# Spreading z over the partitions: one float32 product, or two float32r products of its halves

## Chip, core and metric

The kernel runs on one core of one Trainium2 chip. The metric is the device time of one execution in microseconds (us). Before the change three runs gave 1108.91, 1110.42 and 1110.47 us; the median is 1110.42 us.

## The reference

Random-feature attention over 8 batches, 8 heads, 576 tokens of 64 dimensions with 128 features, then a gated product with two weight matrices and an output matrix:

```python
    q_p, k_p = (phi(q_s), phi(k_s))          # exp(proj - sq - max) / sqrt(m), float32
    kv = np.einsum('bhsm,bhsd->bhmd', k_p, v)
    z = np.sum(k_p, axis=2)
    num = np.einsum('bhsm,bhmd->bhsd', q_p, kv)
    den = np.einsum('bhsm,bhm->bhs', q_p, z)[..., None] + 1e-06
    ...
    return (a * b @ w_out).astype(np.float32)   # a = x @ w_a, b = x @ w_b, x = num / den
```

`z` is the sum of the key features over the tokens of one head: 128 numbers per head. The denominator of every query token is its dot product with `z`.

## The kernel before

**Two kinds of work.** Attention is done by pairs of heads: `pair(u)`, u from 0 to 31, four pairs to a batch. The matrix products after it are done by blocks: `moe_block` for batches 0 and 1, and `moe_block7` (seven products of sub-blocks in place of eight) for batches 2 to 7 and for a last block 8, which holds the 64 left-over tokens of every batch. While block b runs, the pairs of batch b+1 are computed beside it. Blocks 2 to 6 each carry four pairs of the next batch, blocks 7 and 8 carry none.

**Number formats.** The block products split each operand into a rounded float32r part and the float32r rest and make three products (`hi*hi`, `hi*lo`, `lo*hi`). `copier` (L268 on ScalarE, L270 on VectorE) makes the rounded part, `subber` (L276, VectorE) the rest. Attention products are plain float32; the compiler turns each into two TensorE instructions.

**One pair from u = 4 on.** The features of keys (`hk`) and queries (`hq`) come from TensorE (L479), a maximum on VectorE (L502) and an exponential on ScalarE (L515). Then `zadd` (L531) sums the key features over the token chunks with six additions on GpSimd; the result `zs` holds, for each partition, its partial sum of the two heads (128 partitions x 256 numbers). At L540 one float32 product with `ones` (128 x 128, all 1.0) adds the 128 partial sums and puts the total on every partition: `pz`, in PSUM. ScalarE copies it to `zb` (L268). VectorE then makes the denominators `dn` from `hq` and `zb` (L579 to L585), ScalarE scales `hq` (L590), VectorE turns 32x32 blocks (L600), four DMAs write it to `qdr` and one reads it back (L610), and `pm` (L621) is the numerator product, already divided. `split` makes the float32r parts of x from `pm`, and `sums` (L409) the sub-block sums S for `moe_block7`. The pairs 0 to 3 (`u < NFAST`) take another way, `tok_tail`, that has no `zs` and no `pz`. The features lie in a ring of three buffers (`H=3`): a pair needs two, so pair u starts when pair u-2 has read its `hq` in `pm` and pair u-1 its `hk` in `pkv` (L554).

**What sets the order.** Nothing is ordered by hand. `Graph.op` notes each operation with its engine, its cost in ns, its inputs, its buffers and a priority; `Graph.schedule` simulates the five engines and always places the operation that can start first, the lower priority number on a tie. Attention of pair u has priorities near 1000 u, block products start at one million, so attention goes first when both are ready. The order found is then issued; at run time each engine works through its own list in that order. Costs that matter here: `mm4(1, 256)` = 434 ns for the float32 product, `mm(2, 256)` = 240 ns for two float32r products, `act(256)` = 385 ns, `dve(256)` = 416 ns, 738 and 458 ns for the additions on GpSimd, and 70 ns (`LAT`) for each hand-over from one engine to another. `margin` holds an operation back after its inputs are ready: 2200 ns for `pz` (`MARGIN` 1200 + `SUMS` 1000). `GATES` ties the start of the pairs of a batch to units -1, 1, 3 and 5 of the twelve units of a block.

**Output products.** The products `o` (L739) need only the hidden values of a finished unit, so a few of them are always left over and are placed wherever TensorE would wait (`flush`). Twelve groups of three are left over at the end of a block.

Of the kernel before, what the change touches and what calls it, by code (L numbers as in the profile page):

```python
# [7 lines left out]
F32 = mybir.dt.float32  # L8
F32R = mybir.dt.float32r
# [5 lines left out]
X = mybir.AxisListType.X  # L15
PSUM = bass.MemoryType.PSUM

P = 128
B, H, S, D, M = 8, 8, 576, 64, 128
NHP = H // 2  # L20
NU = B * NHP
E, FF = H * D, 1536
NF = FF // P
# [7 lines left out]
VW = D + 2  # L31
# [2 lines left out]
SQ = (0.5 / float(D) ** 0.5) ** 0.5  # L34
EPS = 1e-6 * M

CFG = dict(NFAST=4, H=3, TURN=(7,), BACK=300, AT=2, GATES=(-1, 1, 3, 5), SQPE=4, MARGIN=1200, LOAD=2500, SUMS=1000, JOIN=(0, 1, 2), CONV=(28000, 2600))

# [169 lines left out]
def mm4(n, cols):  # L210
    return n * 2 * max(112, 3 + 0.835 * cols)


def dve(n):
    return 150 + 1.04 * n


def act(n):
    return 165 + 0.86 * n
# [10 lines left out]
@with_exitstack  # L230
def tile_attention_moe(ctx: ExitStack, tc: tile.TileContext, kqt, kqn, vx, omst, idn, wab, wout, out):
    nc = tc.nc
    NFAST, SQPE = CFG["NFAST"], CFG["SQPE"]
    const = ctx.enter_context(tc.tile_pool(name="const", bufs=1))
    sp = ctx.enter_context(tc.tile_pool(name="sp", bufs=1))
    ps = ctx.enter_context(tc.tile_pool(name="ps", bufs=1, space=PSUM))
# [4 lines left out]
        return ap.bitcast(F32)  # L241

    g = Graph()
    for name, n in dict(X=2, Xw=0, nat=2, x2=0, v=2, h=CFG["H"], qd=1, kvz=0, sm=2, sq=2, rd=2, x=4, xa=2, xf=2, S=2, st=0,
                        w=NF, u=NF, t=0, tst=0, wo=3, raw=2, a=2, c=0, bq=0, ghl=2, osb=0, zs=1, z2=1, zb=1, k2=1, kl=2, dn=1, tails=0,
                        at=CFG["AT"], ab=2, o=4).items():
        g.ring(name, n)

    IN_U = dict(st=["u0", "u1"], t=[f"u{k}" for k in range(2, 7)], c=["u7", "u8", "u9"], xa=["u10", "u11"],
                tst=["S0", *(f"u{k}" for k in range(NF))], bq=["a0", "a1"], osb=["raw0", "raw1"])  # L250
# [6 lines left out]
    def fixed(shape, dtype, name):  # L257
        b = g.buf(None, shape, dtype, name)
        b.ap = const.tile(shape, dtype, name=name)
        return b  # L260
# [3 lines left out]
    def copier(o, i, scale=None):  # L264

        def go(e):
            if e == "ACT":
                nc.scalar.copy(o(), i())  # L268
            elif e == "DVE":
                nc.vector.tensor_copy(o(), i())  # L270
            else:
                nc.gpsimd.tensor_scalar(o(), i(), 1.0, 0.0, op0=ALU.mult, op1=ALU.add)
        return go

    def subber(o, i, hi):
        return lambda e: ENG[e].tensor_tensor(o(), i(), f(hi()), op=ALU.subtract)  # L276
# [4 lines left out]

    ident = fixed([P, P], F32, "ident")
    om = fixed([P, M], F32, "om")
    ones = fixed([P, P], F32, "ones")
    junk = fixed([P, M], mybir.dt.bfloat16, "junk")
    ind = fixed([P, 2], F32, "ind")
    for k in range(4):
        g.op({"POOL": 110}, lambda e, k=k: nc.gpsimd.memset(ind.ap[D * (k // 2):D * (k // 2) + D, k % 2:k % 2 + 1], float(k in (0, 3))),
             w=[(ind, k)], prio=-5000)
# [39 lines left out]
    for n, (kind, i, w) in enumerate(units):  # L329
        pr = 4000 + n * 4000 / len(units)  # L330
        more = late[:10] if n < 18 else []
        raw = g.buf("raw", [P, NW], I64 if wide else F32, f"raw{n}", more)
# [3 lines left out]
        if kind == "ab":  # L336
            hb = wab_b[i, w] = g.buf("wu"[i % 2], [P, 2, NC4, P], F32R, f"w{'ab'[w]}{i}")
            v = lambda hb, k: hb.ap[:, k].rearrange("p c f -> p (c f)")
        else:
            hb = wo_b[i] = g.buf("wo", [P, 2, E], F32R, f"wo{i}")  # L340
            v = lambda hb, k: hb.ap[:, k]
# [78 lines left out]

    def pair(u, gate):
        b, hp = divmod(u, NHP)
        nm, pr, fast = f"_{b}_{hp}", 1000 * u, u < NFAST
        more = ["ab0", "ab1", "o0", "o1", "o2", "o3"] if u < NHP else []
        mg = 0 if u < NHP else CFG["MARGIN"]

# [16 lines left out]
        for xb, (c0, c1) in zip(xbs, pieces):  # L443
            g.op({"SP": 330}, dma(lambda xb=xb: xb.ap[:], lambda c0=c0, c1=c1: kqt[b, hp][:, c0 * P:c1 * P]), w=[(xb, None)], alloc=[xb],
                 prio=early, nbytes=P * (c1 - c0) * P * 4)
        h = {}
        if u >= SQPE:
            nat = [g.buf("nat", [P, NCH, D], F32, f"nat{'kq'[w]}{nm}", room) for w in range(2)]
# [6 lines left out]
        if u >= SQPE:  # L455
            sq = g.buf("sq", [P, 2, NCH], F32, f"sq{nm}")
            for w in range(2):
                g.op({"ACT": act(NCH * D)}, lambda e, w=w: nc.scalar.activation(nat[w].ap[:], nat[w].ap[:], AF.Square, scale=SQ),
                     r=[(nat[w], None)], w=[(nat[w], None)], prio=pr, margin=0 if u < 2 * NHP else CFG["LOAD"])
                g.op({"DVE": dve(NCH * D)}, lambda e, w=w: nc.vector.tensor_reduce(sq.ap[:, w], nat[w].ap[:], axis=X, op=ALU.add),  # L460
                     r=[(nat[w], None)], w=[(sq, w)], alloc=[sq] if w == 0 else [], prio=pr)
# [63 lines left out]
        zs = g.buf("zs", [P, 2, M], F32, f"zs{nm}")  # L525
        zb = g.buf("zb", [P, 2, M], F32, f"zb{nm}")
        z2 = g.buf("z2", [P, 2, M], F32, f"z2{nm}")
        pri = pr + 40
# [3 lines left out]
        for j in range(2):  # L532
            c0, tr = 5 * j, slice(TL * j, TL * j + TL)
            zadd("POOL", 2 * M, lambda: z2.ap[:], lambda c0=c0: hk.ap[:, c0:c0 + 2], lambda c0=c0: hk.ap[:, c0 + 2:c0 + 4],
                 [(hk, c0 + i) for i in range(4)], [(z2, None)], [z2, zs] if j == 0 else [])
            zadd("POOL", M, lambda j=j: zs.ap[:, j], lambda: z2.ap[:, 0], lambda: z2.ap[:, 1], [(z2, None)], [(zs, j)])
            zadd("POOL", M, lambda j=j, tr=tr: zs.ap[tr, j], lambda j=j, tr=tr: zs.ap[tr, j], lambda tr=tr: hk.ap[tr, 4],
                 [(zs, j), (hk, 4)], [(zs, j)])
        pz = g.buf("at", [P, 2 * M], F32, f"pz{nm}", more)
        g.op({"PE": mm4(1, 2 * M)}, lambda e: nc.tensor.matmul(pz.ap[:], ones.ap[:], zs.ap.rearrange("p j m -> p (j m)"), start=True, stop=True),  # L540
             r=[(zs, None), (ones, None)], w=[(pz, None)], alloc=[pz, zb], prio=pri + 10, margin=mg and mg + CFG["SUMS"])
        g.op({"ACT": act(2 * M)}, copier(lambda: zb.ap.rearrange("p j m -> p (j m)"), lambda: pz.ap[:]), r=[(pz, None)], w=[(zb, None)], prio=pri + 10)

        k2 = g.buf("k2", [P, M], F32, f"k2{nm}")
# [18 lines left out]
        kl = g.buf("kl", [P, 2, D], F32, f"kl{nm}")  # L563
# [3 lines left out]
        hq = h[1]  # L567

        dn = g.buf("dn", [P, NCH], F32, f"dn{nm}")
        pri = pr + 100  # L570
# [16 lines left out]
        for c in range(NCH):  # L587
# [3 lines left out]
                else:  # L591
                    nc.gpsimd.tensor_scalar(hq.ap[:, c], hq.ap[:, c], dn.ap[:, c:c + 1], None, op0=ALU.mult)
            g.op({"ACT": 392}, scale, r=[(hq, c), (dn, None)], w=[(hq, c)], prio=pri)
        if u in CFG["TURN"]:
            t = pe_transposes(nm, pr, mg, more, hq)
            qT = t, lambda j: t.ap[:, 5 * j:5 * j + 4], lambda j: t.ap[:, 4, TL * j:TL * j + TL]
        else:

            qd = g.buf("qd", [P, 4, NCH, 32], F32, f"qd{nm}")
            g.op({"DVE": dve(NCH * M)}, lambda e: nc.vector.transpose(qd.ap[:], hq.ap.rearrange("p c (j r) -> p j c r", r=32)),  # L600
                 r=[(hq, c) for c in range(NCH)], w=[(qd, None)], alloc=[qd], prio=pr + 110)
            view = lambda: hq.ap.rearrange("p c m -> p (c m)").rearrange("p (i c r) -> p i c r", c=NCH, r=32)


            qdr = qdram[u % 3]
            back = qdram_b[u % 3]

            def spread(e):
                for i in range(4):
                    nc.sync.dma_start(qdr[:, :, i].rearrange("j r n -> r j n"), qd.ap[32 * i:32 * i + 32].rearrange("p j c r -> p j (c r)"))  # L610
            g.op({"SP": 2000}, spread, r=[(qd, None)], w=[(back, None)], prio=-30, nbytes=P * NCH * M * 4)
            g.op({"SP": 400}, dma(lambda: hq.ap.rearrange("p c m -> p (c m)"), lambda: qdr.rearrange("j r i n -> (j r) (i n)")), r=[(back, None)],
                 w=[(hq, None)], prio=-30, nbytes=P * NCH * M * 4, margin=CFG["BACK"])
            qT = hq, lambda j: view()[:, :, 5 * j:5 * j + 4].rearrange("p i c r -> p c i r"), lambda j: view()[:, 2 * j:2 * j + 2, 4]
# [10 lines left out]
        def rest(pt):  # L625
# [2 lines left out]
            g.op({"ACT": act(TL)}, copier(lambda: xT.ap[:, hp, tl], lambda: pt.ap[:, M:M + TL]), r=[(pt, None)], w=[(xT, (hp, b))], prio=pri)  # L628
        me = dict(mm=num, rest=rest, cost=mm4(1, SM) + mm4(1, TL), r=[(kl, None), (qT[0], None)],
                  w=[(pm, None)], alloc=[pm, *xt.new])  # L630
        if hp in CFG["JOIN"]:
            pending.append(me)
        else:
            pt = g.buf("at", [P, M + TL], F32, f"pt{nm}", more)
            g.op({"PE": me["cost"] + 290}, lambda e: num(pt), r=me["r"], w=[*me["w"], (pt, None)], alloc=[pt, *me["alloc"]], prio=pri, margin=mg)
            rest(pt)

    def pe_transposes(nm, pr, mg, more, hq, room=()):

        qb = g.buf("qd", [P, NCH, P], F32, f"qT{nm}", room)  # L640
        for i in range(3):
            pq = g.buf("at", [P, 3 * P], F32, f"pq{nm}{i}", more)

            def go(e, i=i, pq=pq):
                for c in range(3):
                    nc.tensor.transpose(pq.ap[:, c * P:(c + 1) * P], hq.ap[:, 3 * i + c], ident.ap[:])
            g.op({"PE": 3 * 108}, go, r=[(ident, None), *((hq, 3 * i + c) for c in range(3))], w=[(pq, None)], alloc=[pq, qb] if i == 0 else [pq],
                 prio=pr + 110 + 10 * i, margin=mg)
            g.op({"ACT": act(3 * P), "DVE": dve(3 * P) + 100}, copier(lambda i=i: qb.ap[:, 3 * i:3 * i + 3].rearrange("p c t -> p (c t)"), lambda pq=pq: pq.ap[:]),
                 r=[(pq, None)], w=[(qb, i)], prio=pr + 110 + 10 * i)  # L650
        return qb

    def tok_tail(b, hp, nm, pr, mg, more, vb, h, xt):

        hk = h[0]
        kvz = g.buf("kvz", [P, 2, VW], F32, f"kvz{nm}", ["zs0"])
        x32t = g.buf("xf", [P, 4, 2, D], F32, f"x32t{nm}")
        pkv = g.buf("at", [P, 2, 2 * VW + 2], F32, f"pkv{nm}", more)
        heads = [[(0, 0), (1, 1), (2, 2), (3, 3), (4, 4)], [(4, 5), (5, 6), (6, 7), (7, 8), (8, 9)]]
# [9 lines left out]
        g.op({"PE": mm4(10, VW)}, kvmm, r=[(vb, None), (hk, None)], w=[(pkv, None)], alloc=[pkv, kvz], prio=pr + 100, margin=mg)  # L669
        g.op({"ACT": act(2 * VW)}, copier(lambda: kvz.ap[:], lambda: pkv.ap[:, :, 0:VW]), r=[(pkv, None)], w=[(kvz, None)], prio=pr + 100)  # L670
        qT = pe_transposes(nm, pr, mg, more, h[1], ["S1"])
        tails = g.buf("tails", [P, 2, D], F32, f"tails{nm}", ["z20"])
        for j in range(2):
            pn = g.buf("at", [P, 5, WN], F32, f"pn{nm}{j}", more)
            rd = g.buf("rd", [P, 5], F32, f"rd{nm}{j}")
# [338 lines left out]
```

## Time and profile before

| | |
|---|---|
| median of three runs | 1110.42 us |
| profiled execution: time | 1111.44 us |
| profiled execution: span from first to last instruction | 1109.6 us |
| time around the span | 1.84 us |
| TensorE busy | 1088.2 us, 98% |
| VectorE busy | 815.4 us, 73% |
| ScalarE busy | 562.1 us, 51% |
| GpSimd busy | 105.2 us, 9% |
| granted TensorE clock | 0.994 of full |

PE is TensorE's matmul, PEld its weight load, DVE VectorE, ACT ScalarE, POOL GpSimd. Every duration below comes from this one profiled execution. The time around the span does not depend on the kernel's inner order, so a change of the span is carried over to the median as it is. The stages by time: 0 to 97.5 us holds the pairs of batch 0, the start of block 0 and the conversion of the weights; 97.5 to about 201 us the rest of block 0 with the pairs 4 to 7; then block 1 with pairs 8 to 11 to 321.5 us; blocks 2 to 6 of 118.6 to 119.0 us each; blocks 7 and 8 from 915.5 us to the end.

### The profile page before, as it was taken

The page shows a single profiled execution, that of the slowest core. Times are in us where ns is not written, and L with a number is a line of the kernel's source. Part 1 is how long each engine was busy: PE and PEld are TensorE (multiplying, and loading weights), DVE is VectorE, ACT ScalarE, POOL GpSimd, SP SyncE. Part 2 cuts the span into 40 slices and gives each one's busy share as a digit, 9 for nine tenths or more (in the row PEclk, how much of TensorE's full clock was granted, in tenths as well). Part 3 has the DMA queues.
Part 4 walks back from the last instruction along what each step waited for, and adds up shares of the span by engine and source line. Part 5 has one row for each costly group of instructions (what it writes and reads, how often), then busy time and mean ns, then how long its engine had stood idle before and what let it go on. Part 6 is the DMA issues. An engine that isn't in the chain of part 4 may idle for free.

```text
span 1109.6 us, 21421 instructions
## 1 busy us (share of the span) xinstructions
PE 1088.2 (98%) x7717; PEld 938.5 (85%) x7717; DVE 815.4 (73%) x2052; ACT 562.1 (51%) x1544; POOL 105.2 (9%) x176
## 2 busy tenths in 40 slices
PE   8989999999999999999999999999999999999997
PEld 7877777777779888888888898888889889999996
DVE  4799786888978677877697778778877676556544
ACT  5787575766556555554465546564655521002001
POOL 0002010111011111111011111111111100000000
PEclk9899999999999999999999999999999999999999
DMA  9555775697989887888888888888887678777763
GB/s 343 170 196 178 243 226 193 219 341 273 307 284 310 303 285 266 297 287 297 270 268 302 288 284 286 308 294 271 277 298 239 226 260 268 237 245 253 262 226 84
DMA packets 106826, 290.36 MB, mean 262 GB/s; under 512 B 11744, under 2 KB 29664, under 8 KB 106720
## 3 DMA queue, kind: packets, MB, share of 16 engines
q1 hardware_dynamic: 106432, 288.86, 77.2%
q8 instruction: 61, 1.00, 0.3%
q14 instruction: 45, 0.37, 0.1%
q10 hardware_dynamic: 288, 0.13, 0.0%
HBM read 241.57 MB, written 47.38 MB: 260 GB/s over the span
## 4 chain that ended last, share of the span: by engine, by line
PE 86%; DVE 7%; DMA 4%; issue 2%; ACT 1%; SPq 0%; DVEq 0%; ACTq 0%
PE p L875 37%; PE o L739 25%; PE ppk L479 6%; PE pb L785 4%; PE pa L785 4%; PE pkv L554 3%; PE pm L621 2%; DVE raw L315 1%; PE pz L540 1%; DMA raw<-in_wab_dram 1%; DVE sm L502 1%; PE pkv L668 1%; PE ps L492 1%; DMA hq<-qdr 1%; DMA td<-ts 1%
## 5 line engine op out<-in xcount | busy, mean ns | idle before, releaser
L739 PE MATMUL o<-wo,ghl 128*128 128x512 f32 x1296 | 350.7, 399 | 0.0
L885 DVE TENSOR_TENSOR c<-p,c 128x512 f32<-128x512 f32 (+1 forms) x336 | 208.3, 620 | 152.0 <-PE p L875 146.8
L739 PEld LDWEIGHTS o<-wo,ghl 128*128 128x128 f32 x1296 | 226.2, 188 | 38.8
L875 PE MATMUL p<-S,t 128*128 128x256 f32 x1512 | 209.8, 283 | 0.0
L875 PEld LDWEIGHTS p<-S,t 128*128 128x128 f32 x1512 | 194.4, 189 | 9.2
L531 POOL TENSOR_TENSOR z<-hk 128x256 f32<-128x256 f32 x56 | 46.1, 823 | 765.8 <-ACT hk L515 653.5
L479 PE MATMUL ppk<-om,X 64*128 64x128 f32 x576 | 92.0, 295 | 4.3 <-DMA om<-in_omst_dram 3.9
L479 PEld LDWEIGHTS ppk<-om,X 64*128 64x128 f32 x576 | 73.4, 192 | 26.0 <-issue 6.9
L268 ACT COPY c<-p 128x256 f32<-128x256 f32 x84 | 30.9, 368 | 126.2 <-PE p L875 126.2
L590 ACT ACTIVATE hq<-hq,dn 128x128 f32<-128x128 f32 x252 | 78.3, 393 | 32.6 <-DVE dn L585 29.0
L515 ACT ACTIVATE hk<-hk,sm 128x128 f32<-128x128 f32 x216 | 71.6, 393 | 43.6 <-DVE sm L510 42.9
L479 PE MATMUL ppq<-om,X 64*128 64x128 f32 x576 | 91.8, 295 | 0.0
L579 DVE CUSTOM_DVE_ANT_0 junk<-hq,zb 128x128 bf16<-128x128 f32 (+1 forms) x280 | 80.6, 288 | 10.4 <-ACT zb L268 5.9
L785 PE MATMUL pa<-x,wa 128*128 128x512 f32 x288 | 76.3, 405 | 3.1 <-DVE x L276 2.6
L785 PE MATMUL pb<-x,wb 128*128 128x512 f32 x288 | 76.4, 404 | 0.0
L268 ACT CAST ghl<-c 128x512 fp32r<-128x512 f32 x52 | 32.1, 619 | 87.4 <-DVE c L920 86.7
L875 PEld LDWEIGHTS p<-x,t 128*128 128x128 f32 x504 | 69.5, 188 | 6.2
L875 PE MATMUL p<-x,t 128*128 128x256 f32 x504 | 73.9, 282 | 0.0
L875 PE MATMUL p<-S,bq 128*128 128x256 f32 x504 | 73.8, 282 | 0.0
L479 PEld LDWEIGHTS ppq<-om,X 64*128 64x128 f32 x576 | 73.3, 192 | 0.2 <-DVE x L276 0.2
L875 PEld LDWEIGHTS p<-x,wa 128*128 128x128 f32 x504 | 66.4, 188 | 7.8 <-DVE c L885 3.1
L515 ACT ACTIVATE hq<-hq,sm 128x128 f32<-128x128 f32 x216 | 72.5, 390 | 0.0
(120 smaller groups left out, 1644.0 us busy)
## 6 DMA issues: line engine op xcount, KB each, us to landing
t<-td SPq DMA_DIRECT2D x168, 512.0 KB, 4.8
wo<-wod SPq DMA_DIRECT2D x96, 512.0 KB, 5.1
bq<-bd SPq DMA_DIRECT2D x84, 256.0 KB, 5.2
X<-in_kqt_dram SPq DMA_DIRECT2D x28, 576.0 KB, 5.2
qdr<-qd SPq DMA_DIRECT2D x108, 144.0 KB, 3.6
hq<-qdr SPq DMA_DIRECT2D x27, 576.0 KB, 6.2
raw<-in_wab_dram SPq DMA_DIRECT2D x24, 512.0 KB, 4.6
td<-ts SPq DMA_DIRECT2D x24, 512.0 KB, 6.3
```

Source lines behind the costliest of these rows:

```text
L268: nc.scalar.copy(o(), i())
L479: nc.tensor.matmul(pps[w].ap[:, c * M:c * M + M], xcol(3 * i + c)[rows], om.ap[rows], start=True, stop=True)
L515: g.op({"ACT": 392}, lambda e, c=c, w=w, src=src[w]: nc.scalar.activation(h[w].ap[:, c], src(c), AF.Exp, scale=SC, bias=sm.ap[:, 2, w, c:c ...
L531: g.op({"POOL": pool2(n)}, lambda e: ENG[e].tensor_tensor(o(), a(), c(), op=ALU.add), r=r, w=w, alloc=list(al), prio=pri)
L554: nc.tensor.matmul(pkv.ap[D * j:D * j + D, 0:M], vb.ap[:, vc, 0:D], hk.ap[:, c], start=(n == 0), stop=(n == 4))
L579: g.op({"DVE": 413}, lambda e, c=c, j=j, rr=rr: nc.vector.tensor_tensor_reduce(out=junk.ap[rr], in0=hq.ap[rr, c], in1=zb.ap[rr, j], scale= ...
L590: nc.scalar.activation(hq.ap[:, c], hq.ap[:, c], AF.Copy, scale=dn.ap[:, c:c + 1])
L621: nc.tensor.matmul(pm.ap[D * j:D * j + D], kl.ap[:, j], qT[1](j), start=True, stop=True)
L739: nc.tensor.matmul(po.ap[:], ghl.ap[:, gi, t * P:(t + 1) * P], wo.ap[:, wi], start=(n == 0 and i == 0), stop=(n == NF - 1 and i == 2))
L785: nc.tensor.matmul(pb.ap[:], wt.ap[:, wi, c], xs[c].at(xi), start=(c == 0 and i == 0), stop=(c == NC4 - 1 and i == 2))
L875: nc.tensor.matmul(pb.ap[:, half], wcol(wi, c), xc(xi, c), start=n == 0, stop=n == 5)
L885: g.op({"DVE": dve(n)}, lambda e: nc.vector.tensor_tensor(c4.ap[:, o], pb.ap[:, half], y(), op=ALU.add), r=[*((pb, k) for k in range(half. ...
```

## The change

`zs` is no longer multiplied as float32. A new buffer `zr` takes its rounded part (ScalarE, float32r) and the rest (VectorE, `zs` minus the rounded part). `ones` becomes float32r. Two products, one with each half, are added up in the same PSUM tile `pz`. `zr` has one buffer in its ring; its first half is written after the last GpSimd addition, its second after the first. The new operations have a priority number one lower than the product's. `pz` keeps its margin, counted now from the second half of `zr`.

Two small buffers get places of their own: `kvz` and `tails` of the pairs 0 to 3, which lay in the places of `zs` and `z2`. The other lines rename `u < NFAST` into a list of pairs with the same four entries, and add conditions that hold as before for these settings. The planner runs anew with the new costs.

```diff
-CFG = dict(NFAST=4, H=3, ...
+CFG = dict(FAST=(0, 1, 2, 3), JOIN0=False, H=3, ...
...
-    ... qd=1, kvz=0, ... dn=1, tails=0,
+    ... qd=1, kvz=1, ... dn=1, tails=1, zr=1,
...
-    ones = fixed([P, P], F32, "ones")
+    ones = fixed([P, P], F32R, "ones")
...
-        nm, pr, fast = f"_{b}_{hp}", 1000 * u, u < NFAST
+        nm, pr, fast = f"_{b}_{hp}", 1000 * u, u in CFG["FAST"]
...
+        flat = lambda t: t.ap.rearrange("p j m -> p (j m)")
+        zr = g.buf("zr", [P, 2, 2 * M], F32R, f"zr{nm}")
+        hi, lo = (lambda: zr.ap[:, 0]), (lambda: zr.ap[:, 1])
+        g.op({"ACT": act(2 * M)}, copier(hi, lambda: flat(zs)), r=[(zs, None)], w=[(zr, 0)], alloc=[zr], prio=pri + 9)
+        g.op({"DVE": dve(2 * M)}, subber(lo, lambda: flat(zs), hi), r=[(zs, None), (zr, 0)], w=[(zr, 1)], prio=pri + 9)
         pz = g.buf("at", [P, 2 * M], F32, f"pz{nm}", more)
-        g.op({"PE": mm4(1, 2 * M)}, lambda e: nc.tensor.matmul(pz.ap[:], ones.ap[:], zs.ap.rearrange("p j m -> p (j m)"), start=True, stop=True),
-             r=[(zs, None), (ones, None)], w=[(pz, None)], alloc=[pz, zb], prio=pri + 10, margin=mg and mg + CFG["SUMS"])
+
+        def broadcast(e):
+            nc.tensor.matmul(pz.ap[:], ones.ap[:], hi(), start=True, stop=False)
+            nc.tensor.matmul(pz.ap[:], ones.ap[:], lo(), start=False, stop=True)
+        g.op({"PE": mm(2, 2 * M)}, broadcast,
+             r=[(zr, None), (ones, None)], w=[(pz, None)], alloc=[pz, zb], prio=pri + 10, margin=mg and mg + CFG["SUMS"])
...
-        if u in CFG["TURN"]:
-            t = pe_transposes(nm, pr, mg, more, hq)
+        if u < NHP or u in CFG["TURN"]:
+            t = pe_transposes(nm, pr, mg, more, hq, ["S1"] if u < NHP else ())
...
-        if hp in CFG["JOIN"]:
+        if hp in CFG["JOIN"] and u + 1 not in CFG["FAST"] and (u >= NHP or CFG["JOIN0"]):
...
-        kvz = g.buf("kvz", [P, 2, VW], F32, f"kvz{nm}", ["zs0"])
+        kvz = g.buf("kvz", [P, 2, VW], F32, f"kvz{nm}")
...
-        tails = g.buf("tails", [P, 2, D], F32, f"tails{nm}", ["z20"])
+        tails = g.buf("tails", [P, 2, D], F32, f"tails{nm}")
```

## Rows read from the trace of the kernel before

**Rows 1.** The page, parts 1 and 4: busy time, and the chain by line.

```profile
PE 1088.2 (98%) x7717; PEld 938.5 (85%) x7717; DVE 815.4 (73%) x2052; ACT 562.1 (51%) x1544; POOL 105.2 (9%) x176
...
PE p L875 37%; PE o L739 25%; PE ppk L479 6%; PE pb L785 4%; PE pa L785 4%; PE pkv L554 3%; PE pm L621 2%; DVE raw L315 1%; PE pz L540 1%; DMA raw<-in_wab_dram 1%; DVE sm L502 1%; PE pkv L668 1%; PE ps L492 1%; DMA hq<-qdr 1%; DMA td<-ts 1%
```

**Rows 2.** Busy time of each engine by stage; the first row names the columns.

```profile
core 0: us, PE busy (x) PEld busy (x) DVE busy (x) ACT busy (x) POOL busy (x), PEclk, DMA share, GB/s
0.00:97.50 97.50, 88.12 (x617) 75.53 (x617) 72.97 (x179) 71.07 (x185) 5.38 (x14) 0.95 0.67 228
97.50:215.00 117.50, 114.54 (x656) 87.25 (x654) 91.24 (x257) 75.50 (x197) 15.27 (x24) 1.00 0.68 221
215.00:321.50 106.50, 106.32 (x582) 82.07 (x581) 94.52 (x243) 67.12 (x175) 13.86 (x18) 1.00 0.85 292
...
440.50:559.20 118.70, 118.39 (x919) 103.61 (x917) 92.45 (x244) 64.82 (x188) 14.48 (x25) 1.00 0.84 285
```

**Rows 3.** Waits of PE in 440.5:559.2: who waited for whom, us, times, longest.

```profile
PE p L875 <- DVE c L885: 0.3, 1, 0.3
```

**Rows 4.** Busy time once more, one 20 us slice; columns of rows 2.

```profile
80.00:100.00 20.00, 18.92 (x110) 14.48 (x109) 19.86 (x49) 15.85 (x37) 2.40 (x3) 1.00 0.65 200
```

**Rows 5.** The chain that ended last, around pair 31: start us, us, what.

```profile
884.58 0.43 PE pz L540 x2
...
886.51 2.12 PE p L875 x18
```

**Rows 6.** Groups of instructions, shapes apart: xcount, busy us, mean ns, idle before us.

```profile
L531 POOL TENSOR_TENSOR z<-hk 128x256 f32<-128x256 f32 x56 | 46.1, 823 | 765.8 <-ACT hk L515 653.5 <-PE ppq L479 68.8 <-PE o L739 43.6
...
L531 POOL TENSOR_TENSOR zs<-z 128x128 f32<-128x128 f32 x56 | 29.7, 530 | 4.4
L531 POOL TENSOR_TENSOR zs<-zs,hk 64x128 f32<-64x128 f32 x56 | 29.0, 517 | 4.4
...
L276 DVE TENSOR_TENSOR x<-pm,x 128x256 fp32r<-128x256 f32 x12 | 5.1, 424 | 20.1 <-ACT xf L268 13.8 <-PE o L739 6.2
...
L268 ACT CAST x<-pm 128x256 fp32r<-128x256 f32 x12 | 4.4, 366 | 29.3 <-PE pm L621 29.3
...
L268 ACT CAST x<-xT 128x256 fp32r<-128x256 f32 x2 | 0.7, 408 | 0.0
```

**Rows 7.** Timeline at the sums of pairs 20, 21, 23: start us, us, instruction.

```profile
563.01 0.45 POOL L531 TENSOR_TENSOR zs<-zs,hk 64x128 f32<-64x128 f32 x1
...
565.50 0.59 PE L540 MATMUL pz<-zs,ones 128*128 128x256 f32 x2
...
589.17 0.46 POOL L531 TENSOR_TENSOR zs<-zs,hk 64x128 f32<-64x128 f32 x1
...
594.13 0.37 ACT L268 CAST x<-pm 128x256 fp32r<-128x256 f32 x1 [5.26 <-PE pm L621]
...
595.65 0.62 PE L540 MATMUL pz<-zs,ones 128*128 128x256 f32 x2
...
644.94 0.45 POOL L531 TENSOR_TENSOR zs<-zs,hk 64x128 f32<-64x128 f32 x1
...
648.75 0.60 PE L540 MATMUL pz<-zs,ones 128*128 128x256 f32 x2
```

**Rows 8.** Timeline of PE at the ends of blocks 5 and 6.

```profile
795.75 1.08 PE L621 MATMUL pm<-hq,kl 128*64 128x512 f32 x4
...
796.87 3.69 PE L739 MATMUL o<-wo,ghl 128*128 128x512 f32 x15
...
907.77 1.08 PE L621 MATMUL pm<-hq,kl 128*64 128x512 f32 x4 [0.82 <-DMA hq<-qdr]
```

**Rows 9.** Busy time between the pm of pairs 23, 27 and 31; columns of rows 2.

```profile
676.98:795.75 118.77, 118.46 (x917) 103.71 (x917) 92.24 (x244) 64.89 (x187) 14.22 (x24) 1.00 0.84 287
795.75:907.77 112.02, 110.93 (x861) 97.94 (x860) 83.12 (x225) 56.04 (x167) 13.65 (x24) 1.00 0.78 260
```

More of the change, by code (lines that the diff above doesn't have):

```diff
@@ L35 @@
 EPS = 1e-6 * M
-CFG = dict(NFAST=4, H=3, TURN=(7,), BACK=300, AT=2, GATES=(-1, 1, 3, 5), SQPE=4, MARGIN=1200, LOAD=2500, SUMS=1000, JOIN=(0, 1, 2), CONV=(28000, 2600))
+CFG = dict(FAST=(0, 1, 2, 3), JOIN0=False, H=3, TURN=(7,), BACK=300, AT=2, GATES=(-1, 1, 3, 5), SQPE=4, MARGIN=1200, LOAD=2500, SUMS=1000, JOIN=(0, 1, 2), CONV=(28000, 2600))
 class Buf:
@@ L232, in tile_attention_moe @@
     nc = tc.nc
-    NFAST, SQPE = CFG["NFAST"], CFG["SQPE"]
+    SQPE = CFG["SQPE"]
     const = ctx.enter_context(tc.tile_pool(name="const", bufs=1))
@@ L243, in tile_attention_moe @@
     g = Graph()
-    for name, n in dict(X=2, Xw=0, nat=2, x2=0, v=2, h=CFG["H"], qd=1, kvz=0, sm=2, sq=2, rd=2, x=4, xa=2, xf=2, S=2, st=0,
-                        w=NF, u=NF, t=0, tst=0, wo=3, raw=2, a=2, c=0, bq=0, ghl=2, osb=0, zs=1, z2=1, zb=1, k2=1, kl=2, dn=1, tails=0,
+    for name, n in dict(X=2, Xw=0, nat=2, x2=0, v=2, h=CFG["H"], qd=1, kvz=1, sm=2, sq=2, rd=2, x=4, xa=2, xf=2, S=2, st=0,
+                        w=NF, u=NF, t=0, tst=0, wo=3, raw=2, a=2, c=0, bq=0, ghl=2, osb=0, zs=1, z2=1, zb=1, k2=1, kl=2, dn=1, tails=1, zr=1,
                         at=CFG["AT"], ab=2, o=4).items():
```

## The prediction

> **What bounds the kernel now.** I read the busy times first, then the chain by line, then the busy times by stage, then PE's waits. PE is busy 98% of the span, and 37% and 25% of the chain that ended last are the block products p and o [rows 1]. The mean hides two regimes. Up to 97.5 us PE lacks 9.4 us, and up to 215 us another 3.0 us; in the slice 80 to 100 us DVE is busy 19.86 of 20 us, so there DVE is as much the bound as PE [rows 2, 4]. From 215 us on PE is busy 106.32 of 106.50 us, and 118.39 of 118.70 us in block 3, with DVE at 78% and ACT at 55% [rows 2]; PE waited there for other engines once, for 0.3 us [rows 3]. So a TensorE cycle saved in blocks 1 to 6 should be a cycle of the total, if the attention chain beside it does not get too late. Pairs 8 to 31, 24 of the 28 that have a pz, fall into this regime.
>
> The second thing to see is that the attention chain also closes a loop from block to block: pair 3 of a batch ends with its pm, and the next block can only then start. From one such pm to the next it is 118.77 us, with PE busy 118.46 us; in the one period in which no further pair is started beside it, it is 112.02 us, with PE busy 110.93 us [rows 9]. The chain got shorter by 6.75 us where PE had 7.53 us less to do. It stretches and shrinks with PE's load; it does not hold a pace of its own. And right after the pm PE does five groups of left-over o products (15 instructions, 3.69 us) [rows 8]: this is the stock from which a late chain is bridged.
>
> **The change, part by part.**
>
> *The product.* Removed: one float32 product, two PE instructions, 0.43 us on the chain [rows 5], 28 times: 12.0 us. Added: two float32r products of 256 columns with 128x128 weights. The same shape and format are the p products of the blocks: 18 of them in 2.12 us, 0.118 us each [rows 5]. Two take 0.236 us, 28 times 6.6 us. Per pair 0.194 us goes; for 28 pairs 5.4 us, for the 24 pairs in the PE-bound regime 4.7 us. That is the main term. Weight loads do not change in number (two per pair) and run at this pace already in the p products.
>
> *The copy on ACT.* 28 casts of 128x256 to float32r. Nearest rows: 366 ns from PSUM, 408 ns from SBUF [rows 6]; the source here is in SBUF, I take 0.40 us, 11 us in all. ACT is idle 45% of a block [rows 2]. In pair 21 it was idle for 5.26 us up to 594.13, that is through the whole end of the sums [rows 7]. Cost zero; with no cover left it would be 0.40 us a pair.
>
> *The subtraction on DVE.* 28 of 128x256, 424 ns each by the nearest row [rows 6], 12 us. In blocks 2 to 6 DVE has 26 of 119 us free [rows 2], four subtractions take 1.7 us of them. Queued behind it on DVE are the sums c that free p's PSUM halves; between the release of such a sum and the product that needs its half stand twelve products, or six and two o groups, 1.4 us or more (twelve times 0.118), against 0.69 us for the sum: 0.42 us more fit in. Zero there. In the slice 80 to 100 us DVE is full [rows 4], and pair 4's subtraction falls there or just behind: 0 to 0.4 us, I take 0.3.
>
> *The wait added on ACT.* The cast waits for GpSimd's last addition without a margin; before, only PE waited for it, with 2200 ns of margin. Behind it on ACT stand exponentials and the copies c. The planner counts 738 + 458 + 458 ns for the last three additions, the rows give 823 + 530 + 517 on the mean, 0.22 us more [rows 6], but 0.45 and 0.46 us for the last one in blocks 4 and 5 [rows 7]: the excess lies in the early blocks. So ACT stands still for 0 to 0.2 us a pair, at most 28 times 0.2 = 6 us of an engine with 547 us free. The Trainium skill ("TensorE: Matmul & The Clock Gate", Architectural detail) says that ScalarE's and VectorE's queues are strict first-in first-out; by it all of this wait would be passed to what stands behind. By the rows the sum gets nothing from it, by the rule alone up to those 6 us; I go by the rows, since what PE needs of ACT's copies c it needs only after those same 1.4 us.
>
> *The longer way from zs to pz.* Cast, subtraction and two hand-overs: 0.40 + 0.42 + about 0.15 = 1.0 us (an estimate: twice the planner's 0.07 us for a hand-over), less 0.19 us of product. With the margin behind it pz can come about 3.2 us after the last addition. In pair 20 it came 2.04 us after (565.50 less 563.46), in pair 21 6.02, in pair 23 3.36 [rows 7]. So the first pair of a batch loses about 0.9 us, the second and the fourth, which stand in the loop from block to block (pair u waits for the buffers of pair u-2), nothing or a little. What a late pair costs: its pm comes later, at the block's end one or two more of the o groups are placed ahead of it. Between 0 and 0.9 us a block; zero taken, because o products are real work and only their place changes.
>
> *Early pairs 4 to 7.* Their products save 4 x 0.194 = 0.8 us in a stage in which PE is short of work for 3.0 of 117.5 us [rows 2]. Bounds: 0.8 gained, or 1.7 lost if all four subtractions lie on the path. I take 0.5 gained less the 0.3 above: 0.2.
>
> *The rest.* kvz and tails leave places that zs and z2 use first at pair 4, after batch 0 is done: zero. The renamed conditions choose the same pairs: zero. The planner, though, runs with new costs, and every order after the first pz may differ. PE's idle 12.3 us in the first 215 us [rows 2] can be met better or worse by another order; I allow 2 us each way, a sixth of it, and no expected value.
>
> *Sum.* 4.7 + 0.2 = 4.9 us less. The profiled execution of 1111.44 us would become 1106.5; it stands 1.0 us above the median of the runs, so against 1110.42 us the forecast is 1105.5 us.
>
> **The rivals.**
>
> *A: the time is swallowed.* The saved PE time turns into waits, because the loop of the attention chain sets the period of a block. For it: PE's pm of pair 31 waited 0.82 us for the returning DMA [rows 8], and the chain gets the new operations. Against it: the period that shrank with PE's load [rows 9], and 0.3 us of waits in a block [rows 3]. Time: the five periods of blocks 2 to 6 unchanged, only block 1's 0.8 us and the early 0.2 kept: 1109.4 us. The Trainium skill ("Perfetto Trace Analysis", Identifying the Most-Contended Engine) judges TensorE by the busy share of its weight loads and not of its matmuls. That share is 87% in a block [rows 2], which by the rule leaves TensorE some room and speaks for this rival; the rows of the shrunken period speak against it.
>
> *B: slower, through the loop.* If pz of the second and fourth pair also moves by the 0.9 us, the loop gets longer twice a block: 1.8 us for each of five periods, 9 us, against which PE's saving helps nothing there: 1110.4 + 9 - 1 = 1118 us. With one of the two pairs moved it is 1114 us. It decides where pz stands less than about 3.2 us behind the last addition; pair 23 with 3.36 us is at that edge, pair 21 with 6.02 us is far from it [rows 7].
>
> *C: the product is not cheaper.* Were the float32r product with ones run like a float32 one, two would take 0.86 us: 28 x 0.43 = 12 us more, 1122 us. Against it: 0.118 us in every p product [rows 5].
>
> *D: a luckier order.* The early idle time is met better by 2 us: 1103.5 us.
>
> **How the numbers follow.** A measurement of this kernel can tell about 0.2%, 2.2 us, from no change: between 1108.2 and 1112.6 us. The forecast has 0.66 (1103.8 to 1108.2 by the bounds above), D 0.10, A 0.15, B 0.08, C 0.01. Faster: forecast, D and a little of A, 0.78. Same: most of A and the mild half of B, 0.14. Slower: 0.08. Range: 1102.8 to 1109.6 us leaves out B, C, a part of A and the far end of D.
>
> **What would show it.** pz as two instructions about 0.24 us long on the chain, its share down from 12 us to near 7; ACT and DVE up by 11 and 12 us; 56 more casts and subtractions of 128x256 in all; blocks 2 to 6 shorter by 0.8 us each (118.7 to 117.9) with PE still over 99% busy; pz about 3 us or more behind the last addition. The forecast is wrong if the blocks keep their 118.7 us and PE's waits appear at pm or at the block's first S products (rival A), if the period grows (B), or if the total moves by what happens before 215 us.

## The result, and the profile after

The changed kernel takes 1114.43 us (median of 6 runs) against 1110.45 us for the one before (6 runs): ratio 1.0037, interval 1.0024 to 1.0050, so 4.0 us slower. The forecast was 1105.5 us with a range up to 1109.6 us. The profiled execution took 1115.39 us with a span of 1113.6 us, 4.0 us more than before. Three single executions far out of line (2103 us of the kernel before, 3652 and 1502 us in two experiments) are left out of the ratios and medians.

The page of the changed kernel, busy times and chain by line [rows 1]:

```profile
PE 1088.2 (98%) x7717; PEld 936.8 (84%) x7717; DVE 818.0 (73%) x2068; ACT 577.7 (52%) x1584; POOL 108.5 (10%) x176
...
PE p L885 37%; PE o L749 22%; PE ppk L479 6%; PE pa L795 3%; PE pb L795 3%; PE pkv L564 2%; DMA raw<-in_wab_dram 2%; DMA hq<-qdr 2%; PE pm L631 2%; DVE raw L315 1%; DVE sm L502 1%; PE pkv L678 1%; DMA raw<-in_wout_dram 1%; DMA out_dram<-osb 1%; PE ps L492 1%
```

`pz` has gone from the chain (it had 1%), and `hq<-qdr`, the transfer that `pm` waits for, has 2% where it had 1%. PE's busy time is the same to the last digit although its work is 5.4 us less: busy here includes stalls between pipelined products (rows at the end of this section), so it does not show the saving.

The new operations in the groups of the changed kernel, shapes apart (columns of [rows 6]), and the chain around pair 31 [rows 5]:

```profile
L276 DVE TENSOR_TENSOR zr<-zs,zr 128x256 fp32r<-128x256 f32 x28 | 11.8, 421 | 11.4 <-ACT zr L268 10.9
...
L268 ACT CAST zr<-zs 128x256 fp32r<-128x256 f32 x28 | 11.4, 406 | 19.3 <-POOL zs L531 19.2
```

```profile
888.37 1.43 PE p L885 x12
889.79 0.12 PE pz L548
889.91 0.12 PE pz L549
```

Each operation costs what was forecast: 406 ns the cast, 421 ns the subtraction, 0.12 us each product, 0.24 us in place of 0.43. In front of the casts ACT waits 19.2 us in all for GpSimd's sums; how much of that is new is told with the experiments.

Busy time by stage in the changed kernel (columns of [rows 2]):

```profile
97.50:215.00 117.50, 113.03 (x632) 85.07 (x629) 87.93 (x234) 73.01 (x193) 15.16 (x24) 1.00 0.65 211
215.00:321.50 106.50, 105.54 (x598) 81.40 (x595) 94.87 (x261) 69.64 (x186) 13.92 (x18) 1.00 0.83 288
321.50:440.50 119.00, 118.01 (x924) 103.96 (x924) 92.75 (x245) 70.43 (x201) 15.58 (x24) 1.00 0.85 293
440.50:559.20 118.70, 116.95 (x918) 103.04 (x918) 91.07 (x244) 68.28 (x195) 14.54 (x24) 1.00 0.85 294
```

PE lacks 4.5, 1.0, 1.0 and 1.8 us in these stages; before, it lacked 3.0, 0.2, 0.1 and 0.3, by [rows 2] and this row of before:

```profile
321.50:440.50 119.00, 118.92 (x932) 104.96 (x930) 87.47 (x236) 70.76 (x204) 14.73 (x26) 1.00 0.87 293
```

Where the time went is seen at the starts of the blocks (first product p of a block on PE's timeline, us):

```
block                       3       4       5       6       7       8   span
before                  435.4   554.1   672.8   791.8   908.9  1003.2  1109.6
after                   438.7   557.6   676.2   794.2   910.0  1007.0  1113.6
after less before        +3.3    +3.5    +3.4    +2.4    +1.1    +3.8    +4.0
```

By this landmark block 6 lasts 117.1 us before and block 7 starts at 908.9, not 118.6 to 119.0 and 915.5 as in the list of stages.

3.3 us are lost before block 3, 2.4 us come back in blocks 4 to 6, and 2.7 us are lost within block 7. The 3.3 us match PE's idle time from 97.5 to 440.5 us, which grows from 3.2 to 6.4 us (rows above); in the first 97.5 us it falls from 9.4 to 8.0. At the starts of blocks 3 and 7 PE's timeline of the changed kernel looks alike (in brackets the idle time before an instruction and what ended it):

```profile
441.09 3.03 PE L749 MATMUL o<-wo,ghl 128*128 128x512 f32 x12
445.86 1.08 PE L631 MATMUL pm<-hq,kl 128*64 128x512 f32 x4 [1.75 <-DMA hq<-qdr]
...
446.98 1.65 PE L749 MATMUL o<-wo,ghl 128*128 128x512 f32 x6
...
910.66 5.77 PE L749 MATMUL o<-wo,ghl 128*128 128x512 f32 x24
917.01 1.08 PE L631 MATMUL pm<-hq,kl 128*64 128x512 f32 x4 [0.58 <-DMA hq<-qdr]
...
918.13 1.66 PE L749 MATMUL o<-wo,ghl 128*128 128x512 f32 x6
919.63 0.63 PE L885 MATMUL p<-x,wa 128*128 128x256 f32 x4
920.97 0.50 PE L885 MATMUL p<-x,wa 128*128 128x256 f32 x2 [0.71 <-DVE x L276]
```

The `pm` of a batch's fourth pair comes late. PE has done the o products that its list puts ahead of it, 12 and 24 of them, and stands; six more come behind the `pm` in the list. The 1.75 us at 445.86 lie inside block 3 and are no part of the 3.3 us ahead of it; that block lasts 118.9 us, before 118.7. At block 7 this `pm` starts 7.0 us after the block's first product (917.01 less 910.0); before, it stood 1.1 us ahead of it (907.77 in [rows 8], less 908.9). At block 3 it starts 7.1 us after, and before it was 3.9:

```profile
435.38 0.87 PE L875 MATMUL p<-x,wa 128*128 128x256 f32 x6
...
439.32 1.08 PE L621 MATMUL pm<-hq,kl 128*64 128x512 f32 x4
```

The `pm` of pair 11 is late too, at 328.75 us in the changed kernel, before at 309.52.

```profile
328.75 1.08 PE L631 MATMUL pm<-hq,kl 128*64 128x512 f32 x4
```

Of the 2.7 us lost within block 7, 1.3 are idle time of PE. Another part lies inside the busy time: twelve p products in block 7 take 1.57 us before and 1.94 in the changed kernel, with no idle time shown.

```profile
919.55 1.57 PE L875 MATMUL p<-x,wb 128*128 128x256 f32 x12
```

```profile
925.34 1.94 PE L885 MATMUL p<-x,wb 128*128 128x256 f32 x12
```

### The profile page after: what moved, and what is told of

The parts are those of the page before. It is cut to its first block, busy times and chain, and to the rows that moved or that the text cites. A ratio compares the mean times of both kernels' runs of the same rounds, so it can differ in the third digit from the quotient of the medians.

```text
span 1113.6 us, 21434 instructions
## 1 busy us (share of the span) xinstructions
PE 1088.2 (98%) x7717; PEld 936.8 (84%) x7717; DVE 818.0 (73%) x2068; ACT 577.7 (52%) x1584; POOL 108.5 (10%) x176
## 4 chain that ended last, share of the span: by engine, by line
PE 79%; DVE 8%; DMA 7%; ACT 3%; issue 1%; POOL 0%; SPq 0%; ACTq 0%; DVEq 0%
PE p L885 37%; PE o L749 22%; PE ppk L479 6%; PE pa L795 3%; PE pb L795 3%; PE pkv L564 2%; DMA raw<-in_wab_dram 2%; DMA hq<-qdr 2%; PE pm L631 2%; DVE raw L315 1%; DVE sm L502 1%; PE pkv L678 1%; DMA raw<-in_wout_dram 1%; DMA out_dram<-osb 1%; PE ps L492 1%
## 5 line engine op out<-in xcount | busy, mean ns | idle before, releaser
L749 PE MATMUL o<-wo,ghl 128*128 128x512 f32 x1296 | 346.5, 397 | 0.0
L479 PE MATMUL ppk<-om,X 64*128 64x128 f32 x576 | 93.2, 296 | 3.9 <-DMA om<-in_omst_dram 3.6
L589 DVE CUSTOM_DVE_ANT_0 junk<-hq,zb 128x128 bf16<-128x128 f32 (+1 forms) x280 | 83.0, 296 | 13.2 <-ACT zb L268 8.8
L268 ACT CAST ghl<-c 128x512 fp32r<-128x512 f32 x57 | 35.3, 622 | 76.0 <-DVE c L930 75.0
```

Source lines behind the costliest of these rows:

```text
L479: nc.tensor.matmul(pps[w].ap[:, c * M:c * M + M], xcol(3 * i + c)[rows], om.ap[rows], start=True, stop=True)
L589: g.op({"DVE": 413}, lambda e, c=c, j=j, rr=rr: nc.vector.tensor_tensor_reduce(out=junk.ap[rr], in0=hq.ap[rr, c], in1=zb.ap[rr, j], scale= ...
L749: nc.tensor.matmul(po.ap[:], ghl.ap[:, gi, t * P:(t + 1) * P], wo.ap[:, wi], start=(n == 0 and i == 0), stop=(n == NF - 1 and i == 2))
```

## The experiments

All ratios are to the kernel before, with 95% intervals; "+x us" is that ratio on 1110.5 us. A kernel's order is the one that the planner finds for it.

### Instructions or order: three kernels

**The old order with the new operations.** The planner works on the kernel before, with its old cost for the product; the cast and the subtraction are put into its finished list where `zs` is ready.

```diff
...
+        added.append((last, cast, subber(lo, flat, hi)))
         g.op({"PE": mm4(1, 2 * M)}, broadcast,
...
+        steps_all = [(o.start, 0, o.n, o, None) for o in order]
+        for last, cast, sub in added:
+            t = last.end + g.LAT
+            steps_all.append((t, 1, last.n, "ACT", cast))
+            steps_all.append((t + act(2 * M) + g.LAT, 1, last.n, "DVE", sub))
```

> The change's instructions (cast, subtraction, two float32r products) in the order of before: planned with the old costs, the cast and the subtraction put in where zs is ready. Theory ORDER (the new plan's order loses the time): PE's 5.4 us come through, 1105 to 1107 us. Rival WORK (the added instructions, ACT's wait for GpSimd and the longer path lose it in any order): 1112 to 1116 us, as after.

Measured: 1108.15 us, 0.9973 (0.9964 to 0.9982), -3.0 us: 1.2 us above the range of ORDER and 3.9 below that of WORK.

**The new order with the old product.** The changed kernel is planned as it is, but the cast and the subtraction are not issued, and the product is the float32 one of `zs`.

```diff
-    ones = fixed([P, P], F32R, "ones")
+    ones = fixed([P, P], F32, "ones")
...
-        g.op({"ACT": act(2 * M)}, copier(hi, lambda: flat(zs)), r=[(zs, None)], ...
+        g.op({"ACT": act(2 * M)}, lambda e: None, r=[(zs, None)], ...
...
-            nc.tensor.matmul(pz.ap[:], ones.ap[:], hi(), start=True, stop=False)
-            nc.tensor.matmul(pz.ap[:], ones.ap[:], lo(), start=False, stop=True)
+            nc.tensor.matmul(pz.ap[:], ones.ap[:], flat(zs), start=True, stop=True)
```

> The order of after with the instructions of before: cast and subtraction are planned but not issued, the product is the float32 one. Theory ORDER: the time of after plus PE's 5.4 us, less what the missing instructions gave back, 1117 to 1120 us. Rival WORK: the time of before, 1109 to 1112 us.

Measured: 1117.68 us, 1.0059 (1.0047 to 1.0072), +6.6 us. This kernel issues the computation of the kernel before, with not one instruction added, in another order; the two small buffers keep their new places. PE's timeline at block 7 has the same picture as the changed kernel:

```profile
917.76 1.08 PE L630 MATMUL pm<-hq,kl 128*64 128x512 f32 x4 [1.31 <-DMA hq<-qdr]
...
921.71 0.50 PE L884 MATMUL p<-x,wa 128*128 128x256 f32 x2 [0.70 <-DVE x L276]
```

**The old order with the added work only.** As the first, but the product is the float32 one of `zs`; the halves are made and not read.

```diff
-            nc.tensor.matmul(pz.ap[:], ones.ap[:], hi(), start=True, stop=False)
-            nc.tensor.matmul(pz.ap[:], ones.ap[:], lo(), start=False, stop=True)
+            nc.tensor.matmul(pz.ap[:], ones.ap[:], flat(), start=True, stop=True)
```

> The order of before with cast and subtraction issued, but pz made as before by the float32 product of zs: the added work and ACT's wait alone; the halves are not read. Theory WORK2 (the 2.5 us that the old order with the new instructions lacks of PE's 5.4 are lost by the added work): 1112.5 to 1114.5 us. Rival PRODUCT (two float32r products save only about 3 us, the work costs nothing): 1110 to 1111.5 us.

Measured: 1112.37 us, 1.0010 (1.0000 to 1.0019), +1.1 us, between the two ranges. Its waits hold the whole of ACT's new wait, 21.1 us, but ACT's wait for `pm` is shorter than before:

```profile
ACT x L268 <- PE pm L634: 34.0, 13, 4.1
...
ACT zr L268 <- POOL zs L531: 21.1, 21, 1.6
```

and in the kernel before:

```profile
ACT x L268 <- PE pm L621: 47.4, 15, 5.3
```

ACT's idle time as a whole fell from 547.5 us (1109.6 less 562.1) to 539.2 (1110.6 less 571.4), so the new wait stands for the most part where ACT was idle already.

So the instructions as a whole gain 3.0 us in the old order: the cheaper product gains 4.1 (from +1.1 to -3.0; 2.7 to 5.5 by the two intervals), the added work takes back 1.1 (0 to 2.1). The new order loses 6.6 us by itself. 6.6 less 3.0 is 3.6 us, and the change measured 4.0.

### What in the plan makes the order: the margin

In the plan `pz` of the kernel before comes at the earliest 70 + 2200 ns = 2.27 us after the last addition. The changed kernel puts 385 + 70 + 416 + 70 ns in front of that margin: 3.21 us. Five kernels change `SUMS` alone, 1000 ns of those 2200.

```diff
-CFG = dict(FAST=(0, 1, 2, 3), ... SUMS=1000, ...
+CFG = dict(FAST=(0, 1, 2, 3), ... SUMS=0, ...
```

The changed kernel with `SUMS=0`, planned distance 2.21 us:

> The change with SUMS=0 in place of 1000: pz may be planned 1200 ns after zr, so about as long after the last addition as before the change. Theory PATH (it is the longer way from zs to pz, as the planner lays it out, that makes the pairs late): 1105 to 1108 us, and pairs 8 to 11 are back at their old times. Rival CHANCE (any new plan loses the luck of the old settings): 1110 to 1116 us. Rival WORK: 1112 to 1116 us.

Measured: 1105.65 us, 0.9952 (0.9940 to 0.9965), -5.3 us. The `pm` of pair 11 is back at 311.31 us.

The kernel before with `SUMS=2000`, planned distance 3.27 us, no other edit:

> The kernel before with SUMS=2000: pz is planned 1 us later, no instruction is added. Theory PATH: slower than before by 3 to 9 us, 1113 to 1119 us. Rival WORK: 1109 to 1112 us, since nothing is added. CHANCE would leave either.

Measured: 1117.36 us, 1.0062 (1.0048 to 1.0077), +6.9 us. A loss of the same size is there without the change's instructions, again with a late `pm` at block 7 and a longer wait for x behind it:

```profile
917.20 1.08 PE L621 MATMUL pm<-hq,kl 128*64 128x512 f32 x4 [0.86 <-DMA hq<-qdr]
...
922.00 0.80 PE L875 MATMUL p<-x,wa 128*128 128x256 f32 x2 [2.66 <-DVE x L276]
```

It is not lost in the same places. Block 3 starts at 435.2 us here (before 435.4, changed kernel 438.7) and the `pm` of pair 11 is at 311.37; the whole loss lies within block 7, which lasts 100.4 us (before 94.3, changed kernel 97.0).

The kernel before with `SUMS=0`, 1.27 us:

> The kernel before with SUMS=0: pz planned 1 us earlier, nothing else. Theory PATH (time depends on how far behind the last addition the plan puts pz): not slower than before, 1106 to 1111 us. Rival CHANCE (any replanning of these settings loses): 1113 to 1118 us.

Measured: 1109.42 us, 0.9987 (0.9978 to 0.9996), -1.4 us.

The changed kernel with `SUMS=2000`, 4.21 us:

> The change with SUMS=2000: pz planned another 1 us later than in after, about 4.3 us behind the last addition. Theory PATH: slower than after, 1117 to 1124 us. Rival CHANCE: anything from 1106 to 1118 us, no order by distance.

Measured: 1111.11 us, 1.0003 (0.9995 to 1.0012), +0.3 us, 5.9 below the range of PATH. A still longer distance costs less than 3.21 us does, so "the longer, the slower" falls. Here too the `pm` of pair 11 is late, at 324.87 us, and yet block 3 starts at 434.2, earlier than before: late early pairs alone are not a loss.

The changed kernel with `SUMS=500`, 2.71 us:

> The change with SUMS=500: pz planned half-way between the run with 0 and after. Theory PATH as a slope: 1108 to 1112 us; PATH as a step: near 1106 or near 1114. Rival CHANCE: no relation to either.

Measured: 1105.45 us, 0.9948 (0.9934 to 0.9961), -5.8 us.

By planned distance, with 3.0 us added for the kernels that have the change's instructions, so that what is left is the order:

```
planned distance, us   1.27   2.21   2.27   2.71   3.21   3.27   4.21
kernel               before  after before  after  after before  after
order costs, us        -1.4   -2.3    0     -2.8   +7.1   +6.9   +3.3
```

The cost jumps between 2.7 and 3.2 us, in the kernel before between 2.27 and 3.27, and there is no slope. Seven plans show this jump and no rule: beyond it the loss lies in different places, before block 3 and in block 7 in the changed kernel, in block 7 alone at 3.27 us, and at 4.21 us in block 4, which lasts 123.7 us there.

### Which pairs: the second and the fourth

The margin is shortened for some pairs of the changed kernel, or lengthened for some pairs of the kernel before; `hp` is the pair's place in its batch, 0 to 3. First, 1200 ns for the second and fourth pair of the changed kernel, 2200 for the others:

```diff
-             ... margin=mg and mg + CFG["SUMS"])
+             ... margin=mg and mg + (0 if hp % 2 else 1000))
```

> The change with the margin of pz shortened by 1 us for the second and fourth pair of a batch only. Theory LOOP (what counts is the path of the pairs that stand in the loop from block to block, second and fourth): as with SUMS=0 for all, 1104 to 1107 us. Rival START (the first and third pair, whose pz moved most, make the rest late): 1111 to 1116 us, like after.

Measured: 1104.35 us, 0.9941 (0.9927 to 0.9955), -6.6 us, the lowest median of all (that of `SUMS=500` is within the noise of it) and faster than both kernels. On PE's timeline the `pm` of pair 31 is at 896.14 us and block 7 starts at 903.00:

```profile
896.14 1.08 PE L631 MATMUL pm<-hq,kl 128*64 128x512 f32 x4 [0.65 <-DMA hq<-qdr]
...
903.00 1.56 PE L885 MATMUL p<-x,wa 128*128 128x256 f32 x12
```

The same for the first and third pair, `(0 if hp % 2 == 0 else 1000)`:

> The change with the margin of pz shortened by 1 us for the first and third pair of a batch only. Theory LOOP: like after, 1111 to 1117 us. Rival START: 1104 to 1107 us.

Measured: 1112.83 us, 1.0016 (1.0007 to 1.0025), +1.8 us.

In the kernel before, 1000 ns more for the second and fourth pair, `(2000 if hp % 2 else 1000)`:

> The kernel before, nothing added, with pz planned 1 us later for the second and fourth pair of a batch only. Theory LOOP: as with 1 us for all pairs (e4), 1114 to 1119 us. Rival CHANCE (which pairs are late does not matter, the change's own plan is an unlucky one): no relation, most likely within 2 us of before.

Measured: 1120.0 us, 1.0075 (1.0062 to 1.0089), +8.3 us, 1.0 us above the range of LOOP.

And for the first and third, `(1000 if hp % 2 else 2000)`:

> The kernel before with pz planned 1 us later for the first and third pair only. Theory LOOP: 1108 to 1112 us, no loss. Rival START (the pairs whose pz the change moved most): 1113 to 1118 us.

Measured: 1111.9 us, 1.0007 (0.9998 to 1.0016), +0.8 us, not told from no change. The two kernels differ in one wait at the start of block 7; waits from 880 to 960 us, of the kernel with the second and fourth pair late, then with the first and third:

```profile
PE p L875 <- DVE x L276: 2.9, 1, 2.9
```

```profile
PE p L875 <- DVE x L276: 0.7, 1, 0.7
```

The changed kernel has a wait of 0.7 us there too, so this wait is not the mark of the loss. In both kernels here the `pm` of pair 31 is late, 8.4 and 6.4 us after block 7's first product, and block 7 lasts 100.2 and 96.5 us (before 94.3); but the one with the first and third pair late reaches block 7 2.4 us earlier than before, at 906.5 us, and so ends even.

Four kernels agree: the second and fourth pair carry most of it, with either sign, in either kernel. The first and third take a smaller part: 4.0 in the changed kernel less 1.8 with their margin short is 2.2, by the intervals anything from 0.5 to 4.

### Where: before block 3 and at block 7

The short margin of 1200 ns for all pairs, but only for u below 12, `(0 if u < 12 else 1000)`:

> The change with the margin shortened for pairs 4 to 11 only; from pair 12 on it is that of after. Theory END (the loss sits in pairs that come late at the ends of blocks 2 to 6): 1111 to 1115 us. Rival FRONT (it sits in blocks 0 and 1, where pairs 8 to 11 come 13 to 17 us late in after): 1105 to 1108 us. Both in part: 1108 to 1111 us.

Measured: 1109.17 us, 0.9986 (0.9977 to 0.9994), -1.6 us.

Only for u from 12 on, `(1000 if u < 12 else 0)`:

> The reverse: margin of after for pairs 4 to 11, shortened from pair 12 on. Theory END: 1105 to 1108 us. Rival FRONT: 1111 to 1115 us. Both in part: 1107 to 1111 us.

Measured: 1109.45 us, 0.9990 (0.9982 to 0.9999), -1.1 us. Against the short margin everywhere (-5.3), a long one for the late pairs alone costs 3.7 us, for the early ones alone 4.2; the change has both and stands 9.3 us above it. Block 3 starts at 434.2 us in the early-short kernel and at 437.0 in the late-short one; block 7 lasts 97.7 us and 92.8. Busy time of PE in two stretches (columns of [rows 2]), of the early-short kernel, then of the late-short one:

```profile
160.00:480.00 320.00, 317.96 (x2141) 262.17 (x2140) 259.53 (x698) 199.56 (x546) 41.22 (x66) 1.00 0.83 283
...
880.00:1000.00 120.00, 117.99 (x831) 107.53 (x830) 71.11 (x143) 22.51 (x54) 0.24 (x1) 1.00 0.75 249
```

```profile
160.00:480.00 320.00, 314.63 (x2105) 259.38 (x2103) 258.04 (x686) 198.20 (x541) 43.59 (x66) 1.00 0.82 280
...
880.00:1000.00 120.00, 118.74 (x842) 109.49 (x841) 71.25 (x140) 20.09 (x49) 0.00 (x0) 1.00 0.77 253
```

And of the changed kernel, and the one with the second and fourth pair short:

```profile
160.00:480.00 320.00, 313.48 (x2093) 257.55 (x2092) 257.03 (x677) 196.87 (x538) 43.85 (x66) 1.00 0.81 278
...
880.00:1000.00 120.00, 118.54 (x828) 107.68 (x828) 74.01 (x150) 24.65 (x60) 1.65 (x3) 1.00 0.75 252
```

```profile
160.00:480.00 320.00, 319.26 (x2165) 263.82 (x2166) 261.54 (x705) 201.11 (x549) 41.41 (x66) 1.00 0.83 285
...
880.00:1000.00 120.00, 119.35 (x834) 110.59 (x833) 73.68 (x131) 21.26 (x50) 0.00 (x0) 1.00 0.76 247
```

PE idles 5 to 7 us in 160 to 480 us where the early pairs are long (320 less 314.63 and 313.48), 0.7 to 2 us where they are not; from 880 to 1000 us the early-short kernel idles 2.0 us and the late-short one 1.3. The second difference is small; by the block starts above each half of the changed kernel's loss sits where its pairs are planned.

Over all sixteen kernels the length of block 7 goes with where the `pm` of pair 31 starts, counted from the block's first product: 92.8 to 93.2 us where it is 6.9 us ahead, 94.3 to 94.5 at 1.1 ahead, 95.2 to 97.7 at 5.8 to 7.8 behind, 100.2 to 100.4 at 8.4 to 8.7 behind. No run moved this `pm` alone.

## Why the prediction was wrong

**The product: right in its size; where the time is gained, only in part.** 0.24 us for 0.43 us, as forecast. 4.9 us of gain were summed; the old order with and without it gives 4.1 (1.0010 less 0.9973, each with an interval of about 0.0009 either way), which does not differ from the sum by more than the noise. That a TensorE cycle saved in the steady blocks is a cycle of the total is borne out less well. Between those two kernels blocks 3 to 6 shrink by 1.4 us in all, where sixteen pairs should save 3.1, and 3.5 us are gained before block 3 (it starts at 432.6 and 436.0 us, block 7 at 905.0 and 909.8; one profiled execution each). In the changed kernel blocks 5 and 6 last 118.0 and 115.8 us where they lasted 119.0 and 117.1; block 4 kept its length (118.6 for 118.7).

**The cast, the subtraction and ACT's wait: near the sum, the bound on the wait wrong.** I had bounded ACT's stall at 6 us; its wait for the sums is 19.2 us in the changed kernel and 21.1 in the old order, most of it where ACT was idle before. Cast, subtraction and wait together cost 1.1 us (0 to 2.1) against the 0.3 in the sum, which the interval holds. The rule of the Trainium skill ("TensorE: Matmul & The Clock Gate", Architectural detail), that ScalarE's queue is strict first-in first-out, is neither borne out nor refuted: no row here tells whether ready work was held up behind a cast.

**The step that failed: "The longer way from zs to pz".** It came to "zero taken", as a lag of about 1 us on the chip that o products bridge. The second step that failed is "I allow 2 us each way, a sixth of it, and no expected value" for the planner's new order. They were one step. The longer way acts in the plan: there it moves `pz` from 2.27 to 3.21 us behind the last addition, past a jump between 2.7 and 3.2 us, and the planner then makes another order, worth +6.6 us with the old instructions. I had priced the extra lead as if the order stayed, and the order as if it were chance. That lead alone, as margin in the unchanged kernel, gives +6.9 us, all of it at block 7.

On the chip the lag that I had priced is not what is lost. I had 0.9 us for the first pair of a batch and nothing or a little for the second and fourth. `pz` of pair 20 stood 2.04 us behind its last addition before [rows 7] and stands 4.13 behind in the changed kernel; pair 21 has 3.27 (at 598.07 us) for 6.02, pair 23 3.18 for 3.36. The first pair is later than priced, the two in the loop are not. In the early blocks whole pairs move: `pz` of pair 8 starts at 219.69 us, before at 206.93, and in the kernel with the short second and fourth margins at 204.91; but in the kernel before with `SUMS=2000` at 205.57, so the longer lead alone does not make the early pairs late.

**"O products are real work and only their place changes"** held while the list had o products to place. At blocks 3 and 7 those ahead of the late `pm` are done, and PE stands 1.75 and 0.58 us for `hq<-qdr`; at block 7 those behind it too, and PE stands 0.71 us for x. I had seen the stock in [rows 8] and not asked when it is empty. I had also read that the next block can only start after this `pm`: six products of block 3 start 3.9 us ahead of it before (435.38 and 439.32).

**The rivals.** B had the right sign, pairs (second and fourth) and edge (3.2 us), and a price of 4 to 8 us; its way, a period longer in each block by pairs moved on the chip, was not it, and that its 1114 us was met is luck: the periods of blocks 3 to 6 did not grow as it has them (118.9, 118.6, 118.0 and 115.8 us for 118.7, 118.7, 119.0 and 117.1). A does not explain the loss, since blocks 5 and 6 gained; that in the old order less than half of the saving came out in blocks 3 to 6 speaks for a part of it. D, a luckier order, exists and is larger than its 2 us: the kernel with the short second and fourth margins is 6.6 us faster than before, 3.6 more than the instructions give.

**What stays open.** Why the planner's order is bad just beyond the jump and less so at 4.21 us, what beside the longer lead makes the changed kernel lose before block 3, and why the second and fourth pair decide: that their buffers and `pm` close the loop to the next block fits the late `pm` rows, but no run changed the ring of the features or the gates. Which single decision of the planner turns is not known.

## What to carry to other kernels

When a list scheduler plans the order, price a change as two: the new instructions in the old order, and the new order with the old instructions; each is one kernel to run, and here they were -3.0 and +6.6 us. When operations are put ahead of one that has a safety margin, take what they add out of the margin first; here 1000 ns less for two pairs in four turned a loss of 4.0 us into a gain of 6.6. And look at where the fill work runs out, not only at whether there is some.

## What was not expected of the hardware

PE's busy time was 1088.2 us before and after, with 5.4 us less of products, while the span grew by 4.0 us: the stalls are partly inside the busy time (twelve products in 1.94 us that took 1.57), so the start times of the blocks had to be read in its place. A new wait in the list of waits need not be new idle time: in the old order ACT waited 21.1 us for GpSimd's sums, its idle time as a whole fell by 8.3 us, and the time rose by 1.1 us (0 to 2.1).
